# Fourteen warm-up products of 128x128 pieces become twelve steps of four 64x64 pieces over 256 columns

## The chip, the cores and the metric

The kernel runs on one core of a Trainium2 chip. The metric is the device time of one execution in microseconds; lower is better. Before the change the median of three runs is 920.34 us (920.31 to 920.46).

A core has five engines that run side by side and meet only at semaphores: TensorE (PE) for matrix products, VectorE (DVE), ScalarE (ACT), GpSimd (POOL), and SyncE (SP), which here only issues DMA transfers. The profile shows the weight load that goes with each matrix product in a row of its own, PEld.

## What is computed

Two blocks follow each other. The first is an attention in which queries and keys are replaced by products of two small projections; the second sends every row of the result through eight small two-layer networks and mixes their outputs with weights from eight rounds of row and column normalisation.

```python
def phi(x):                       # q, k: (4, 4, 1088, 32); S1, S2: (8, 32)
    a = np.einsum('rd,bhsd->bhsr', S1, x)
    b = np.einsum('rd,bhsd->bhsr', S2, x)
    return np.einsum('bhsi,bhsj->bhsij', a, b).reshape(*x.shape[:-1], r * r)
q_p, k_p = (phi(q), phi(k))
kv = np.einsum('bhsf,bhsd->bhfd', k_p, v)
z = np.sum(k_p, axis=2)
attn = (q_p @ kv) / (q_p . z + 1e-06)          # shortened
...
x = attn as (4352, 128)
P = np.exp(x @ w_gate - max)                   # (4352, 8)
for _ in range(8):
    P /= P.sum(1, keepdims=True) + 1e-09
    P /= P.sum(0, keepdims=True) + 1e-09
    P *= N / E
for e in range(E):                             # w1: (128, 1024), w2: (1024, 128)
    out += P[:, e:e + 1] * (np.maximum(x @ w1[e], 0.0) @ w2[e])
```

All of it is in float32.

## The kernel before

**The large part.** Nearly all the time goes to the eight networks. `first` (the product at L914) multiplies a piece of w1 by up to 512 columns of the transposed activations, in two products that stand beside each other in the array: each has 64 columns of weights, and `tile_position=(0, 0)` or `(0, 64)` says which half of the array's columns it takes. ACT applies the maximum with zero (L918), DVE forms sums and differences (L931, L978), and `into` (L1099) multiplies by w2 or by sums of its pieces. The generator `steps` lays this stream out, and the call `fill(n)` hands out n steps of it between pieces of the attention and of the routing, so that PE has work while those wait.

**The order.** The body of the kernel is recorded inside `tc.manual_schedule`, first for DVE, PE and ACT, then for DVE and PE: on these engines the instructions stand in the order in which they are written. POOL and SP keep the order that the scheduler gives them.

**The start.** Before that body the kernel issues the two small loads of S1 and S2, and POOL fills a 128x128 tile `ones` (L111). PE then runs the loop at L113 and L114: fourteen products of `ones` by `ones` into one PSUM bank, `warm`. Nobody reads `warm`. The tile comes from the pool `aps`, which has four PSUM banks that are handed out in turn (`bank()` takes one, too). POOL clears small tiles, and SP issues the loads of k, q and v.

The first useful work follows in the order of the code at the end of the kernel:

- `projections` (DVE, L34 to L260): turns S1 and S2 into the weights `wd`.
- `transpose_k(0, halves)` (DVE, L302 twice, then L304) and `transpose_q(0, ...)` (DVE, L297): bring k and q into the layout that PE needs.
- `keys_ab(0, halves)` (PE, L314 and L319; ACT, L317 and L320): sixteen products and one more of 64 columns, copied out by ACT into `ab`. `halves` cuts them in two parts of eight, each with a bank of its own; L319 has a third bank.
- `query_products(0)` (PE, L376): four products of 64 rows by 128 columns of weights over 512 columns; two of them stand beside each other in the array's rows, `tile_position=(64 * i, 0)`. Each of the two goes to another PSUM bank.
- `keys_products(0, part)` (DVE, L331): the products of a and b for the keys, into `kp`.
- `keys_sums(0)` (PE, L347): 36 products of `kp` with v; `keys_kept` (ACT, L362) copies them out.
- `fractions(0, ...)` (PE, L392), `queries_ab(1)` (PE, L426), and then the first steps of the large stream.

Queries of later batches go out through DRAM to be repeated: `queries_ab` stores them from SP and POOL (L433, L437), and `repeat_a`, `repeat_b` (SP, L443, L446) load them again as `ph` and `rb`. DVE multiplies these (L453), and PE uses the product at L462.

`logits` (PE, L496) is used further on as a row for comparison: four products of 32 columns of weights each, `tile_position=(0, 32 * b)`, over 512 or 288 columns.

Each float32 product of the code appears in the profile as two weight loads and two matmul instructions; the fourteen products are 28 of each.

Of the kernel before, what the change touches and what calls it, by code (L numbers as in the profile page):

```python
# [10 lines left out]
F32 = mybir.dt.float32  # L11
# [39 lines left out]
def kernel(  # L51
# [12 lines left out]
    nc = tc.nc  # L64
    P = nc.NUM_PARTITIONS
# [19 lines left out]
    aps = ctx.enter_context(tc.tile_pool(name="aps", bufs=4, space=PSUM))  # L85
# [23 lines left out]

    ones = consts.tile([P, P], F32, name="ones")  # L110
    nc.gpsimd.memset(ones, 1.0)  # L111
    warm = aps.tile([P, 512], F32, tag="a", name="a")
    for _ in range(14):  # L113
        nc.tensor.matmul(warm[:, 0:P], ones, ones, start=True, stop=True)  # L114
    own = consts.tile([P, H], F32, name="own")
    nc.gpsimd.memset(own, 0.0)
    for h in range(H):
# [1153 lines left out]
```

## Time and profile before

| | |
|---|---|
| median of three runs | 920.34 us (920.31 to 920.46) |
| the profiled execution, first to last instruction (span) | 918.0 us |
| that execution's own time beyond the span | not given by the profile; the median is 2.3 us above the span |
| PE busy | 911.2 us, 99% of the span |
| DVE busy | 678.9 us, 74% |
| ACT busy | 421.6 us, 46% |
| POOL busy | 204.0 us, 22% |
| the warm-up products at L114 | 28 matmul instructions, starting from 1.0 to 6.9 us |
| start of the first product that uses data (L314) | 7.19 us |

Times within the profile are counted from the first instruction. The busy time of PE says only that some product is in the array: the profile models the ends of matmuls, and two or four products beside each other count once. What a product costs in a dense stream is therefore read from the distance between the starts of equal products. "x8" after a group is the number of instructions in it; of a float32 product these are two. The form "128*64 128x256" means 128 rows by 64 columns of weights, and 256 columns streamed through them.

### The profile page before, as it was taken

Reading aid. Unit: us, or ns where it says so; the run is one execution under the profiler, and the core shown is the slowest. Engines: PE = TensorE matmul, PEld = TensorE weight load, DVE = VectorE, ACT = ScalarE, POOL = GpSimd, SP = SyncE. Lnnn points to the kernel's source line nnn. Section 1 sums busy time; section 2 is a strip of 40 time slices with the busy share of each in tenths; the row PEclk is TensorE's granted clock in tenths of the full one; section 3 lists DMA queues with packets and bytes.
Section 4 is the critical chain, followed back from the end, with each engine's and each line's share of the span. In section 5 each row is a group of like instructions: output and inputs, shape, how many; then the busy total and the mean of one; then the engine's idle time right before and its main releaser. Section 6 shows DMA issues by size and latency. Waiting matters only on the chain.

```text
span 918.0 us, 18893 instructions
## 1 busy us (share of the span) xinstructions
PE 911.2 (99%) x7442; PEld 637.4 (69%) x7442; DVE 678.9 (74%) x1173; ACT 421.6 (46%) x915; POOL 204.0 (22%) x212
## 2 busy tenths in 40 slices
PE   9999999999999999999999999999999999999997
PEld 6777544466666677777777777777777655556886
DVE  7678699888776798666975656956567976758665
ACT  3455555554444454444544444544445444445443
POOL 3121100175545421201210010110100243210220
PEclk9999999999999999999999999999999999999999
DMA  9994100213454535534364343454445456453640
GB/s 254 308 273 163 54 1 1 70 64 127 148 150 139 186 119 174 165 110 150 114 185 134 117 143 112 132 187 127 133 122 165 130 170 195 162 166 92 177 153 13
DMA packets 91305, 128.15 MB, mean 140 GB/s; under 512 B 25392, under 2 KB 69504, under 8 KB 86480
## 3 DMA queue, kind: packets, MB, share of 16 engines
q1 hardware_dynamic: 88384, 121.42, 42.7%
q0 software_dynamic: 1600, 5.36, 2.1%
q8 instruction: 58, 0.95, 0.4%
q10 hardware_dynamic: 1232, 0.16, 0.1%
q14 instruction: 31, 0.25, 0.1%
HBM read 107.88 MB, written 19.05 MB: 138 GB/s over the span
## 4 chain that ended last, share of the span: by engine, by line
PE 97%; DVE 2%; ACT 1%; issue 0%; POOL 0%; DVEq 0%; POOLq 0%
PE a L914 51%; PE s L1099 41%; PE a L347 1%; PE a L462 1%; PE a L114 1%; DVE hb L931 1%; PE a L314 0%; PE s L376 0%; PE a L426 0%; PE s L392 0%; DVE cs L602 0%; PE a L496 0%; PE a L392 0%; ACT hb L918 0%; DVE rs L596 0%
## 5 line engine op out<-in xcount | busy, mean ns | idle before, releaser
L914 PE MATMUL a<-xe,w 128*64 128x256 f32 (+1 forms) x2560 | 569.8, 470 | 0.0
L918 ACT ACTIVATE hb<-a 128x256 f32<-128x256 f32 (+4 forms) x408 | 195.0, 480 | 241.5 <-PE a L914 209.3
L914 PEld LDWEIGHTS a<-xe,w 128*64 128x64 f32 x2560 | 263.0, 137 | 50.8 <-issue 1.8
L918 ACT ACTIVATE hx<-a 128x256 f32<-128x256 f32 (+1 forms) x360 | 167.3, 465 | 213.5 <-PE a L914 191.6
L1099 PE MATMUL s<-hb,ws 128*64 128x256 f32 (+3 forms) x1312 | 256.1, 395 | 0.2 <-DVE hb L931 0.2
L1099 PE MATMUL s<-hx,ws 128*64 128x256 f32 x1280 | 233.9, 379 | 0.0
L978 DVE TENSOR_TENSOR hb<-hb 128x512 f32<-128x512 f32 (+1 forms) x204 | 133.5, 664 | 102.8 <-ACT hb L918 98.8
L978 DVE TENSOR_TENSOR hx<-hx 128x512 f32<-128x512 f32 (+1 forms) x204 | 149.8, 744 | 65.0 <-ACT hx L918 60.2
L1099 PEld LDWEIGHTS s<-hb,ws 128*64 128x64 f32 x1312 | 134.9, 137 | 87.8 <-issue 64.5
L678 POOL TENSOR_TENSOR xe<-xT,xe 128x768 f32<-128x768 f32 (+2 forms) x41 | 80.3, 1958 | 481.2 <-DMA xe<-pT 377.0
L1099 PEld LDWEIGHTS s<-hx,ws 128*64 128x64 f32 x1280 | 132.7, 137 | 71.6 <-issue 50.3
L914 PE MATMUL a<-xT,w 128*64 128x416 f32 (+3 forms) x512 | 119.7, 462 | 0.0
L1099 PE MATMUL s<-hb,w 128*64 128x256 f32 (+3 forms) x536 | 114.2, 408 | 0.0
L1099 PE MATMUL s<-hx,w 128*64 128x256 f32 x384 | 76.0, 379 | 0.0
L931 DVE TENSOR_TENSOR hb<-hb 128x416 f32<-128x416 f32 (+7 forms) x84 | 60.7, 723 | 18.0 <-ACT hb L918 14.0
L1099 PEld LDWEIGHTS s<-hb,w 128*64 128x64 f32 x536 | 54.1, 137 | 19.0 <-issue 6.5
L914 PEld LDWEIGHTS a<-xT,w 128*64 128x64 f32 x512 | 48.9, 137 | 25.5 <-issue 15.7
L242 POOL TENSOR_TENSOR ws<-w 128x256 f32<-128x256 f32 (+1 forms) x70 | 60.5, 899 | 8.1 <-DMA w<-in_moe_w_dram 5.2
L931 DVE TENSOR_TENSOR hx<-hx 128x256 f32<-128x256 f32 (+1 forms) x65 | 39.5, 612 | 24.0 <-ACT hx L918 22.8
L1099 PEld LDWEIGHTS s<-hx,w 128*64 128x64 f32 x384 | 40.8, 137 | 6.6
L978 DVE TENSOR_TENSOR pqg<-hb 128x512 f32<-128x512 f32 x68 | 40.5, 637 | 0.0
L978 DVE TENSOR_TENSOR pqg<-hx 128x512 f32<-128x512 f32 x68 | 35.0, 554 | 0.0
(181 smaller groups left out, 485.0 us busy)
## 6 DMA issues: line engine op xcount, KB each, us to landing
w<-in_moe_w_dram SPq DMA_DIRECT2D x82, 512.0 KB, 5.5
ws<-ws SPq DMA_DIRECT2D x34, 1024.0 KB, 5.0
xe<-pT SPq DMA_DIRECT2D x34, 384.0 KB, 4.1
ws<-ws SPq DMA_DIRECT2D x12, 512.0 KB, 3.6
ph<-qa SPq DMA_DIRECT2D x12, 288.0 KB, 4.7
rb<-qb SPq DMA_DIRECT2D x3, 1152.0 KB, 7.2
pb<-pT SPq DMA_DIRECT2D x6, 384.0 KB, 8.3
kx<-in_k_dram SPq DMA_DIRECT2D x4, 544.0 KB, 4.0
```

What stands on the lines that cost most here:

```text
L114: nc.tensor.matmul(warm[:, 0:P], ones, ones, start=True, stop=True)
L242: tc.keep_in_program_order(nc.gpsimd.tensor_tensor(ws[:, c:c + len(ns)], blocks(x), blocks(y), op=Alu.subtract if off else Alu.add))
L347: nc.tensor.matmul(pv[64 * s:64 * (s + 1), i], kp[0:n, H * t + h].rearrange("p i j -> p (i j)"), vx[0:n, slots[h], t, :], start=(t == 0 an ...
L462: nc.tensor.matmul(pn[64 * s:64 * (s + 1), t, 2 * i:2 * i + 2].rearrange("p h d -> p (h d)"), ph[:, i, s, 64 * t:64 * (t + 1)], kvs[b % 2] ...
L678: tc.keep_in_program_order(nc.gpsimd.tensor_tensor(out, x, pb, op=Alu.mult))
L914: nc.tensor.matmul(ph[sl], loaded_w[j][0][:, P * f + H2 * s:P * f + H2 * (s + 1)], sources[j][:, lo:hi], start=True, stop=True, tile_posit ...
L918: nc.scalar.activation(out=out, in_=ph, func=Act.Relu)
L931: nc.vector.tensor_tensor(out, a, b, op=Alu.subtract)
L978: nc.vector.tensor_tensor(out if not isinstance(out, tuple) else places(*out), places(*a), places(*b) if isinstance(b, tuple) else b, op=A ...
L1099: nc.tensor.matmul(sums[g][i][H2 * s:H2 * (s + 1), n * place:n * (place + 1)], w, x, start=c == 1, stop=c == per, tile_position=(0, H2 * s))
```

## The change

The loop of fourteen products is replaced. Two PSUM banks of `aps` are taken for `warm` instead of one. Twelve steps follow, each of four products: the 64x64 quarters of `ones` are the weights, `tile_position=(64 * r, 64 * c)` puts each quarter in its own quarter of the array, and the columns streamed are 256 copies of the first column of `ones`, read again and again. The two quarters of one row half write to the two halves of the partitions of one bank; the other row half has the other bank. Again nobody reads `warm`.

```diff
     ones = consts.tile([P, P], F32, name="ones")
     nc.gpsimd.memset(ones, 1.0)
-    warm = aps.tile([P, 512], F32, tag="a", name="a")
-    for _ in range(14):
-        nc.tensor.matmul(warm[:, 0:P], ones, ones, start=True, stop=True)
+    warm = [aps.tile([P, 512], F32, tag="a", name="a") for _ in range(2)]
+    for _ in range(12):
+        for r in range(2):
+            for c in range(2):
+                rows, cols = slice(64 * r, 64 * (r + 1)), slice(64 * c, 64 * (c + 1))
+                nc.tensor.matmul(warm[r][cols, 0:256], ones[rows, cols], ones[rows, 0:1].to_broadcast([64, 256]),
+                                 start=True, stop=True, tile_position=(64 * r, 64 * c))
```

In the built program, PE's list has 48 products at this place instead of 14. Every other instruction of every engine stands where it stood. One wait is added: the product at L319, whose bank is now the first of the two of `warm`, waits for PE's own warm-up to have ended.

## The prediction

> **What bounds the kernel.** I read the page first: which engine is full, and what the chain that ended last is made of.
>
> ```profile
> PE 911.2 (99%) x7442; PEld 637.4 (69%) x7442; DVE 678.9 (74%) x1173; ACT 421.6 (46%) x915; POOL 204.0 (22%) x212
> PEclk9999999999999999999999999999999999999999
> PE 97%; DVE 2%; ACT 1%; issue 0%; POOL 0%; DVEq 0%; POOLq 0%
> ```
>
> PE is the bound over the whole span: 97% of the chain lies on it. So a microsecond that PE starts its useful work later is a microsecond at the end, unless PE has a later wait on something that does not move. The chain of waits over the first 11 us shows where that useful work starts:
>
> ```profile
> 0.74 0.20 POOL ones L111
> ...
> 1.00 6.26 PE a L114 x28
> 7.26 1.08 PE a L314 x32
> 8.34 0.11 PE a L319 x2
> 8.45 1.92 PE s L376 x8
> 10.37 2.42 PE a L347 x72
> ```
>
> The 28 warm-up instructions lie on this chain from 1.00 us, and L314 follows them directly. Was L314 waiting for them or for its data? DVE's timeline has the answer:
>
> ```profile
> 5.30 0.35 DVE L260 TENSOR_TENSOR wd<-st,own 128x64 f32<-128x64 f32 x1
> 5.58 1.29 DVE L302 STREAM_TRANSPOSE kT<-kx 128x512 f32<-128x512 f32 x2
> 6.80 0.20 DVE L304 STREAM_TRANSPOSE kT<-kx 128x64 f32<-128x64 f32 x1
> 7.04 0.71 DVE L297 STREAM_TRANSPOSE qT<-qx 128x512 f32<-128x512 f32 x1
> 8.33 1.22 DVE L331 TENSOR_TENSOR kp<-ab 128x1024 f32<-128x1024 f32 x1 [0.58 <-ACT ab L317]
> ```
>
> The weights wd are there at 5.65, the first half of kT at about 6.23, the second at 6.87. PE was the last to be ready. But the gain behind an earlier end is small: L331 cannot start before DVE has finished L297 at 7.75, and it started at 8.33. So an earlier end of the warm-up is worth 0.58 us at most, while a later one costs in full.
>
> **At what pace PE runs.** The clock row prints full speed everywhere, but the products say otherwise at the start:
>
> ```profile
> L114 PE MATMUL a<-ones x28: 341/421/582, 1.0 to 6.9; 128*128 128x128 f32 x28
> 2.65 2.55 PE L114 MATMUL a<-ones 128*128 128x128 f32 x11
> ```
>
> The second line is PE's timeline from 3 to 5 us: eleven instructions fill 2.55 us, of which the last one alone takes 0.42, so ten distances between starts are 2.13 us, 0.213 us for 128 columns. Later 256 columns need hardly more: the chain gives four instructions of L914, two pairs beside each other, 0.43 us, so 0.216 us for 256 columns. The warm-up runs at half the full pace. L314's 16 pairs start from 7.19 to 8.11, 0.06 us a pair for 64 columns, which is nearly the full pace (64/256 of 0.216 is 0.054). The pace doubles about 7 us after the start, and the trace's own clock record bears it out: its first entry, full speed, starts at 7.05 us; the views print 1.00 where there is no entry.
>
> **The change part by part.** Removed: 28 instructions of 0.213 us, all in the open. Added: 48 products, 96 instructions over 256 columns. What four quarters beside each other cost is not in the trace, but two neighbours are. L496 has four products side by side in columns, L376 two side by side in rows:
>
> ```profile
> 106.11 0.64 PE L496 MATMUL a<-xT,wg 128*32 128x512 f32 x4
> ...
> 8.38 0.70 PE L376 MATMUL s<-qT,wq 64*128 64x512 f32 x2
> ```
>
> The first comes from a window of 0.2 us, the second from one of 0.15 us: four, and two, instructions start together; the next four of L496 begin at 106.56, the next pair of L376 at 8.92, then 9.35, 9.77, so 0.42 to 0.45 us for 512 columns, the pace of a single stream. Columns and rows both overlap, so I take four-fold overlap: 96 instructions are 24 groups of 256 columns, each 0.427 us at the half pace (twice 0.213) and 0.216 at the full. From the other side: if only two of the four overlap, there are 48 groups. Neither row is like that, so I take 24 and keep 48 as a rival.
>
> The moment of the doubled pace is the second unknown. Between bounds: at the start of the products (24 x 0.216 = 5.2 us, end at 6.2 us, before the data, so 0.58 us gained) and never during them (24 x 0.427 = 10.2 us). The nearest row is L114 itself, an array as full as the new one, from the same start: doubling at 7.05 us. The sum: first start 1.00; the first instruction took 0.16 us longer than its successors (1.00 to 1.37), so 1.16. Until 7.05: 5.89 / 0.427 = 13.8 groups. Left: 10.2 groups at 0.216 = 2.2 us, to 9.25. The turn from row halves to column halves costs about 0.10 us (L376's last pair at 9.77 plus 0.43, L347 at 10.30), so L314 starts at 9.35 instead of 7.19: 2.16 us later.
>
> What does the delay meet? Behind the warm-up on PE stand L314, L319, L376; ACT waits for L314 to fill ab, DVE for ab (L331), PE's L347 for kp, ACT for L347, PE's L392 for ACT (a wait of 0.6 us): each of these is released by the one before, so they all move by the same amount. Stores and reloads of ab through DRAM (L433 to L446) move as a whole, too, as do the loads queued behind them on SP; the ones ahead of them do not move and finish relatively earlier, so DMA can only be less in the way. On PE's own list of waits there are 0.6 us for ACT, 0.2 for DVE and the 1.0 at the start; none is for a transfer with a fixed date, so nothing takes the 2.16 us back. I cost the remaining edits at nothing: the second bank is taken from four when none of the others is in use, which turns the later hand-outs by one place; the wait added to L319 is for products that ended sixteen products earlier on the same engine. If that cover failed, the price would be one drain, 0.1 us.
>
> Sum, on the profiled execution: 918.0 + 2.2 = 920.2 us; the median of the runs lies 2.3 us higher, so 922.5.
>
> Two rules of the Trainium skill speak against the change. The page "TensorE: Matmul & The Clock Gate", Part 1, says the clock is lifted after a busy window of 3.413 us that runs freely, so it is a matter of time and not of the number of products. The clock record agrees in one point: it lasts 911.36 us, 267.0 such windows. By that page alone the doubling could come, by the phase of the window, between about 4.4 and 7.8 us (one to two windows after the first start), and my sum would lie between +0.9 and +2.5 us; as an estimate it makes the spread wider, not its sign. The same page, Part 3, says a weight load overlaps a running product only in another row group; by that, one load in each group would stand in the open, 24 x 0.14 = 3.3 us more. The row of L914, loads of 137 ns and still 0.43 us for four, shows no such cost.
>
> **The rivals.** (1) The clock rises earlier, since four weight sets and two streams for each row half look busier than one. For it: nothing in this trace excludes that the measure counts tiles. Against it: the array is as full in L114. Price with the doubling half way, at 4.0 us: 6.7 groups by then, 17.3 x 0.216 = 3.74, end at 7.74, L314 at 7.84: +0.65 us, 921.0, not slower by 0.2%. It decides from a doubling before about 6.4 us, where the sum falls under 1.84 us. (2) The pieces do not lift the clock while they run: end at 1.16 + 10.2 = 11.4 us, L314 at 11.5, +4.3 us, 924.6; and if the work behind needed another 6 us at half pace, 3 us on top, 927.6. Against it is the full array again. (3) The quarters overlap only in twos: 48 groups, 34.2 left at 7.05 us, 7.4 us, end at 14.4, L314 at 14.5, +7.3, 927.6. Against it: both rows above. (4) The change does nothing, because a later wait takes the delay: for it speak only short waits of ACT and DVE after 130 us; 920.3 to 921.
>
> **How the numbers follow.** A measurement of this kernel tells 0.2% from no change, 1.84 us. My forecast, doubling near 7 us with four-fold overlap, gets 0.60, with its own range 921.6 to 922.9 (a doubling between 5.2 and 7.9 us: 0.49 us later for each microsecond); 0.50 of it lies above 922.18, since the row that fixes 7.05 is a direct one. Rival 1 gets 0.25, rival 2 0.07, rival 3 0.05, rival 4 0.03. Slower by more: 0.50 + 0.07 + 0.05 = 0.62. Within: 0.10 + 0.25 + 0.01 = 0.36. Faster by more would need 1.84 us where the data allow 0.58; I leave 0.02 (out of rival 4) for what I do not see. The range 920.8 to 924.7 leaves out rival 3, the long half of rival 2 and the earliest part of rival 1, some 0.15.
>
> **What would show it.** In the profile after: 96 instructions at the warm-up's line, starting in fours; 0.43 us between fours until about 7 us and 0.22 after; last start near 9.0; L314 at 9.3 to 9.4, L331 at about 10.5. The span is 920.2, and the products after 166 us take as long as before. A first start of L314 near 7.8 with fours 0.22 us apart from 4 us on is rival 1; fours that never come closer than 0.43 us are rival 2; pairs are rival 3. If L314 is 2 us late and the span is not, the statement that nothing takes it back was wrong.

## The result: 1.1 us slower, half of what was forecast

Over 18 runs of each, the changed kernel takes 921.30 us in the median (920.16 to 925.5) and the kernel before 920.23 us (919.18 to 921.34). The ratio is 1.0015 with a 95% interval of 1.0009 to 1.0021: slower beyond doubt, by 1.1 us, which is less than the 0.2% that was called measurable and half of the 2.16 us of the forecast. The time lies in the range that was given.

The page of the changed kernel, its parts 1 and 2, against the rows shown of before:

```profile
PE 913.1 (99%) x7510; PEld 596.8 (65%) x7510; DVE 685.0 (74%) x1173; ACT 421.2 (46%) x915; POOL 211.0 (23%) x212
PEclk9999999999999999999999999999999999999999
```

PE is as full as before; the span has grown from 918.0 to 919.9 us. The chain of waits of the changed kernel (start, length, what; lines have moved down by four: L117 is the warm-up, L318 was L314, L380 was L376, L351 was L347):

```profile
1.00 8.17 PE a L117 x96
9.16 1.08 PE a L318 x32
...
10.36 1.92 PE s L380 x8
12.28 2.42 PE a L351 x72
```

The warm-up holds 8.17 us of the chain instead of 6.26. The products behind it have their old lengths and stand 1.9 us later: L318 starts at 9.10 instead of 7.19. The same 1.9 us are between the two traces at the first product of the large stream (19.31 against 17.41), at its last (914.55 against 912.65) and at the end (919.9 against 918.0); on the way the distance varies by a few tenths (2.0 at L462, which starts at 36.02 against 34.04). Nothing took it back in this execution.

PE's timeline of the changed kernel, from two windows (4.4 to 6.2 us, 6.59 to 8.6 us); a group also holds the instructions that still run when the window opens:

```profile
4.04 2.73 PE L117 MATMUL a<-ones 64*64 64x256 f32 x24
...
6.17 2.78 PE L117 MATMUL a<-ones 64*64 64x256 f32 x44
```

The 24 instructions of the first line are six fours with starts from 4.04 to 6.17, 0.427 us apart; within a four the starts lie at most 0.02 us apart, so all four quarters run at once. The 44 of the second line are eleven fours; from 6.60 on they are 0.22 us apart. The trace's clock record starts at 6.59 us.

DVE's timeline of the changed kernel holds something that the profile of before did not show:

```profile
6.71 1.30 DVE L306 STREAM_TRANSPOSE kT<-kx 128x512 f32<-128x512 f32 x2 [1.06 <-DMA kx<-in_k_dram]
7.93 0.20 DVE L308 STREAM_TRANSPOSE kT<-kx 128x64 f32<-128x64 f32 x1
8.06 0.67 DVE L301 STREAM_TRANSPOSE qT<-qx 128x512 f32<-128x512 f32 x1
```

The load of k came 1.06 us later than DVE was ready for it; before, DVE started at 5.58 with no wait. No instruction of that load was changed. In the changed kernel this cost nothing, since L318 still had to wait for the warm-up.

### The profile page after: what moved, and what is told of

Same layout as the page of the kernel before. It is cut to its first block, busy times and chain, and to the rows that moved or that the text cites. A ratio compares the mean times of both kernels' runs of the same rounds, so it can differ in the third digit from the quotient of the medians.

```text
span 919.9 us, 19030 instructions
## 1 busy us (share of the span) xinstructions
PE 913.1 (99%) x7510; PEld 596.8 (65%) x7510; DVE 685.0 (74%) x1173; ACT 421.2 (46%) x915; POOL 211.0 (23%) x212
## 4 chain that ended last, share of the span: by engine, by line
PE 98%; DVE 1%; issue 0%; ACT 0%; POOL 0%; DVEq 0%; POOLq 0%
PE a L918 56%; PE s L1103 37%; PE a L351 1%; PE a L117 1%; PE a L466 1%; PE a L318 0%; PE s L380 0%; DVE hb L935 0%; PE a L430 0%; PE s L396 0%; PE a L500 0%; PE a L396 0%; DVE cs L606 0%; DVE rs L600 0%; DVE y L794 0%
## 5 line engine op out<-in xcount | busy, mean ns | idle before, releaser
L918 PE MATMUL a<-xe,w 128*64 128x256 f32 (+1 forms) x2560 | 692.1, 470 | 0.0
L918 PEld LDWEIGHTS a<-xe,w 128*64 128x64 f32 x2560 | 320.4, 137 | 112.8 <-issue 1.6
L1103 PE MATMUL s<-hb,ws 128*64 128x256 f32 (+3 forms) x1312 | 331.6, 395 | 0.2 <-DVE hb L935 0.2
L1103 PE MATMUL s<-hx,ws 128*64 128x256 f32 x1280 | 306.3, 379 | 0.0
L1103 PEld LDWEIGHTS s<-hb,ws 128*64 128x64 f32 x1312 | 158.4, 137 | 70.2 <-issue 14.2
L1103 PEld LDWEIGHTS s<-hx,ws 128*64 128x64 f32 x1280 | 154.5, 137 | 57.3
L1103 PE MATMUL s<-hb,w 128*64 128x256 f32 (+3 forms) x536 | 134.4, 408 | 0.0
L1103 PE MATMUL s<-hx,w 128*64 128x256 f32 x384 | 95.7, 380 | 0.0
L1103 PEld LDWEIGHTS s<-hb,w 128*64 128x64 f32 x536 | 60.5, 137 | 23.4 <-issue 6.5
L982 DVE TENSOR_TENSOR pqg<-hb 128x512 f32<-128x512 f32 x68 | 46.5, 723 | 0.0
```

The lines of the kernel that those rows point to most:

```text
L918: nc.tensor.matmul(ph[sl], loaded_w[j][0][:, P * f + H2 * s:P * f + H2 * (s + 1)], sources[j][:, lo:hi], start=True, stop=True, tile_posit ...
L982: nc.vector.tensor_tensor(out if not isinstance(out, tuple) else places(*out), places(*a), places(*b) if isinstance(b, tuple) else b, op=A ...
L1103: nc.tensor.matmul(sums[g][i][H2 * s:H2 * (s + 1), n * place:n * (place + 1)], w, x, start=c == 1, stop=c == per, tile_position=(0, H2 * s))
```

## The experiments

Twelve runs were made on four chips, and each group had its own runs of the kernel before beside it. "Moment" is the time at which the trace's clock record begins, the doubled pace; "first" is the start of the first useful product (L314 of before). The median includes what lies outside the span of an execution, the time from its first to its last instruction.

| run | against the kernel before | median, us | moment | first |
|---|---|---|---|---|
| e1, changed kernel again | 1.0012 (1.0003 to 1.0021) | 921.48 | 6.48 | 9.04 |
| e2, seven steps of quarters | 1.0009 (0.9998 to 1.0020) | 921.00 | 4.81 | 6.41 |
| e3, twelve whole products of 256 columns | 1.0008 (1.0000 to 1.0017) | 921.15 | 5.58 | 8.64 |
| e4, no warm-up | 1.0017 (1.0007 to 1.0027) | 921.60 | 12.54 | 7.11 |
| e5, kernel before again | 0.9999 (0.9991 to 1.0008) | 920.20 | 5.14 | 7.02 |
| e6, before, k later | 1.0013 (1.0004 to 1.0022) | 921.02 | 4.20 | 8.17 |
| e7, changed, k later | 1.0014 (1.0005 to 1.0023) | 921.48 | 7.06 | 9.32 |
| e8, twenty-four steps | 1.0070 (1.0058 to 1.0083) | 926.76 | 4.87 | 13.48 |
| e9, before, k in two halves | 1.0010 (1.0002 to 1.0019) | 920.86 | 5.07 | 7.49 |
| e10, the same, eleven products | 1.0014 (1.0005 to 1.0023) | 921.71 | 5.11, and again 11.94 | 8.82 |
| e11, seven steps of quarters again | 1.0010 (1.0001 to 1.0019) | 921.07 | 5.67 | 6.96 |
| e12, seven whole products of 256 columns | 1.0001 (0.9992 to 1.0010) | 920.28 | 5.09 | 6.48 |

**e1, the changed kernel again.** No edit.

> The changed kernel once more, as the yardstick for the other runs of this chip. Theory of length (the warm-up costs the time that PE spends in it beyond the moment when k and q are ready; what kind of product fills it does not matter): 0.9 to 1.5 us over the kernel before; the start of the first useful product is 0.49 times the moment of the doubled pace plus 5.87 us, so between 8.0 and 9.8 us, with the moment between 4.4 and 7.9 us. Theory of kind (the quarters themselves lift the clock later, or turn the array at a price): the same time, but the moment would often lie beyond 7.9 us.

1.06 us over the kernel before, as in the first measurement. The formula of the expectation is the sum of the forecast with the moment left open. The moment is 6.48 us, and 0.49 x 6.48 + 5.87 gives 9.05 us for the first product; it started at 9.04.

**e2 and e11, seven steps of quarters**, as long at the half pace as the fourteen products:

```diff
-    for _ in range(12):
+    for _ in range(7):
```

> Only the number of steps differs from the changed kernel: seven steps of four quarters, 14 groups of 0.427 us at the half pace, 5.97 us, the same as the fourteen whole products of the kernel before. Theory of length: the time of the kernel before, within 0.3 us. Theory of kind: most of the loss stays, 0.7 to 1.1 us over the kernel before.

> The seven steps of quarters once more, since their interval held both theories. Theory of length: the time of the kernel before, ratio 1.000 within 0.0006. Theory of kind: ratio 1.0009 to 1.0015, as the twelve steps.

The medians are 0.6 and 0.9 us over the kernel before. The first interval holds both theories, the second just leaves out no change. By the medians the theory of length was missed twice, and the theory of kind was met in e11 and just missed in e2.

The spans on record say otherwise. Their medians are 918.9 and 918.7 us, in both runs 0.3 over the kernel before on the same chip (918.6 and 918.4), which the theory of length allows. The rest lies outside the span: 2.0 to 3.0 us in eight of these 22 executions, where the other fourteen and every execution of the kernel before have 1.7 to 1.9.

The two traces, too, show nothing of the quarters in the start: the first products began at 6.41 and 6.96 us, after the warm-up had ended and as soon as kT was there, earlier than the 7.19 of the kernel before. What e11's profiled execution lost, it lost elsewhere, most of it at the last stores: its last product of the large stream starts at 913.02 us and the end comes 6.3 us later, where the other traces have 5.3 to 5.4. The four last stores of ACT's queue, in before and in e11, take 1.91 and 2.96 us to issue:

```profile
913.56 1.91 ACTq L872 DMA_DIRECT2D out_dram<-yt  x4
```

```profile
913.93 2.96 ACTq L876 DMA_DIRECT2D out_dram<-yt  x4
```

**e3, whole products as long as the twelve steps:**

```diff
-    for _ in range(14):
-        nc.tensor.matmul(warm[:, 0:P], ones, ones, start=True, stop=True)
+    for _ in range(12):
+        nc.tensor.matmul(warm[:, 0:256], ones, ones[:, 0:1].to_broadcast([P, 256]), start=True, stop=True)
```

> Only the length differs from the kernel before: twelve whole products of 128x128 over 256 columns, 24 instructions of 0.427 us at the half pace, as long as the twelve steps of quarters. Theory of length: the time of the changed kernel, within 0.3 us (0.8 to 1.4 us over the kernel before). Theory of kind: the time of the kernel before, within 0.3 us.

The chain of e3, in the kernel's old line numbers:

```profile
0.99 7.71 PE a L114 x24
8.71 1.08 PE a L314 x32
```

The moment was 5.58 us, the sum 0.49 x 5.58 + 5.87 gives 8.6 us, and L314 started at 8.64: a quarter of the instructions, the same length. The median is 0.7 us over the kernel before, just under what was expected, and its interval begins at no change.

**e4, no warm-up**, the loop and `warm` left out:

> The warm-up is left out; what it computed was read by nobody. Theory of length: the first useful product starts when k is ready, at 6.3 to 7.4 us, and runs at half the pace until the clock rises, which PE's activity from there on brings about 3.4 to 7 us later; about half of that is lost: 1 to 3.5 us over the kernel before, and the doubled pace is seen only after 10 us. If the kernel before had its clock from somewhere else than the warm-up: 0 to 0.6 us faster than the kernel before.

```profile
1.51 4.81 DMA kx<-in_k_dram
...
6.34 0.72 DVE kT L299
...
7.11 1.97 PE a L311 x32
9.08 0.21 PE a L316 x2
9.29 3.55 PE s L373 x8
```

Here the chain is the load of k. The 32 instructions of the first product's line take 1.97 us instead of 1.08 and the eight of the next take 3.55 instead of 1.92: half the pace, until the moment at 12.54 us. The cost is 1.2 us. So fourteen products are worth 1.2 us, and twelve steps of quarters give back nearly all of it: with 921.48 us on the same chip their median is only 0.1 us better than without a warm-up.

**e5, the kernel before against itself.** No edit.

> The kernel before against itself, for the noise and for a second look at its start. Ratio 1.000 within 0.001. Theory of two spreads (the moment of the doubled pace lies anywhere between about 4.4 and 7.9 us, and the load of k lands up to 1.1 us later in some executions): the profile's own moment of the doubled pace will not be 7.05 us again, and the first useful product starts between 6.3 and 8.0 us, set by whichever ends last of the warm-up and the load. If both are fixed to the start of the kernel: 7.05 us and 7.19 us again, within 0.05.

Its chain:

```profile
1.50 4.72 DMA kx<-in_k_dram
...
6.25 0.72 DVE kT L302
...
7.02 1.28 PE a L314 x32
```

The same program, and another start: the moment at 5.14 us instead of 7.05, the warm-up over 0.7 us before L314, and L314 set by the load of k, which landed at 6.23. In the first profile of this kernel, k was there before 5.58 and the warm-up was the last to end. Both are spreads of single executions, not properties of the kernel.

The earlier start did not make e5 shorter: its span is 918.4 us against 918.0. The turning of q on DVE (L297) comes behind that of k, and the next products (L376, L347) stand where they stood before, within 0.04 us. Then the repeated queries come back through DRAM 0.5 us later than in the first profile, and L462 stands 0.35 us later. Before, and then e5:

```profile
32.79 1.83 DVE L453 TENSOR_TENSOR ph<-ph,rb 128x768 f32<-128x768 f32 x2 [4.56 <-DMA rb<-qb]
34.04 0.87 PE L462 MATMUL a<-kvs,ph 128*64 128x66 f32 x24
```

```profile
33.33 1.83 DVE L453 TENSOR_TENSOR ph<-ph,rb 128x768 f32<-128x768 f32 x2 [5.06 <-DMA rb<-qb]
34.39 0.92 PE L462 MATMUL a<-kvs,ph 128*64 128x66 f32 x24
```

**e6 and e7, k issued after the first piece of q**, in the kernel before and in the changed one:

```diff
-    load_k(0)
     load_q(0, 0, 16)
+    load_k(0)
```

> The kernel before with the first piece of q issued ahead of k, so that k lands 0.5 to 1.3 us later. Theory (in the kernel before, a late k is in the open): 0.3 to 1.2 us over the kernel before, and the first useful product waits for k. If k has slack there: no change, within 0.2 us.

> The changed kernel with the same exchange of loads. Theory (the long warm-up hides a late k, so part of what it costs was already lost in the kernel before): the time of the changed kernel, 0.9 to 1.4 us over the kernel before and within 0.3 us of it; the first useful product starts right after the warm-up, at 0.49 times the moment of the doubled pace plus 5.87 us. If the late k added to it: 1.5 to 2.5 us over the kernel before.

The chain of e6, and then, from another view, the chain of e7:

```profile
2.35 5.03 DMA kx<-in_k_dram
...
7.40 0.72 DVE kT L302
...
8.17 1.28 PE a L314 x32
```

```profile
1.00 8.40 PE a L117 x96
9.39 1.08 PE a L318 x32
```

In both, DVE had k at 7.4 us. The kernel before pays for it, 1.0 us in the median, with L314 at 8.17. The changed kernel does not show it at its start, with the warm-up alone on the chain: its long warm-up covers a late k. Its median is 1.4 us over the kernel before of this chip, at the upper edge of what was expected, where e1 has 1.1 on its chip; the two intervals overlap. This execution also answers the forecast directly: its moment is 7.06 us, the value that the forecast assumed, and L318 starts at 9.32 where 9.35 was forecast; the span is 920.2 us, as forecast.

**e8, twice the steps**, `range(24)`:

> Twice the steps. Theory of length: the twelve steps more all run at the full pace, 24 groups of 0.216 us, 5.2 us over the changed kernel and 6.1 to 6.7 us over the kernel before; the first useful product at 0.49 times the moment of the doubled pace plus 11.05 us. If later waits take back part of a late start of PE: clearly less, 3 to 5 us.

```profile
1.00 12.55 PE a L117 x192
13.55 1.08 PE a L318 x32
```

Moment 4.87 us, 0.49 x 4.87 + 11.05 = 13.4, and L318 started at 13.48. Against e1's profile the first product starts 4.4 us later and the span ends 4.5 us later (924.6 against 920.0). The median of five executions is 6.7 us over the kernel before, 5.3 over the 921.48 of e1 and of e7 where the sum gives 5.2; two of the five have 0.5 and 1.0 us of it outside the span. A long delay of PE's start goes to the end in full.

**e9 and e10, the first k in two halves from two queues**, an attempt at a faster kernel:

```diff
-    load_k(0)
+    kx0 = ld.tile([P, SA, D], F32, tag="k", name="kx", bufs=1)
+    for i, queue in enumerate((nc.sync, nc.scalar)):
+        queue.dma_start(out=kx0[64 * i:64 * (i + 1)],
+                        in_=k[0, 2 * i:2 * (i + 1)].rearrange("h (s a) d -> (h s) a d", a=SA))
+    loaded["k", 0] = kx0
```

> The kernel before with its load of the first k in two halves, one from SP and one from ACT's queue, so that k is issued 0.4 us sooner. Theory (the first useful product of the kernel before waits in many executions for k): k lands 0.2 to 0.8 us earlier and the time falls by 0.2 to 0.6 us. If the transfer is bound by the DMA engines and not by its issue: no change, within 0.2 us.

> The same with eleven whole products instead of fourteen, 4.7 us at the half pace, an end at 5.85 us at the latest. Theory of length: with an early k, the first useful product starts at 6.3 to 6.4 us, 0.3 to 0.9 us under the kernel before. Against it: where the doubled pace comes after 5.85 us the work behind runs up to 1 us at the half pace, which gives back up to 0.5 us.

DVE's timelines of e9 and of e10:

```profile
6.72 1.31 DVE L306 STREAM_TRANSPOSE kT<-kx 128x512 f32<-128x512 f32 x2 [1.07 <-DMA kx<-in_k_dram]
```

```profile
8.05 1.30 DVE L306 STREAM_TRANSPOSE kT<-kx 128x512 f32<-128x512 f32 x2 [2.18 <-DMA kx<-in_k_dram]
```

Both expectations failed. In the timelines SP's half takes 0.81 us to issue, as long as the whole k did in e5 (0.80), so this half was issued no sooner; ACT's half was, by 0.3 us (1.43 + 0.61 against 1.50 + 0.80). k landed no earlier, at about 6.7 and 8.0 us. In e10 that puts the first product at 8.82 us.

e10's profiled execution, the slowest of its eleven (922.87 us), shows what a warm-up that ends long before the data risks. PE was done with it at 5.67 us and stood idle for 3.15 us. The clock record falls back to half speed at 8.53 us and returns to full at 11.94, so the first useful products run at half the pace, 1.98 us instead of 1.08 (a row for 9 to 11 us, in which the third number from the end is the clock, and a row of the chain):

```profile
9.00:11.00 2.00, 2.00 (x36) 1.88 (x35) 1.68 (x4) 0.53 (x2) 0.00 (x0) 0.50 1.18 227
```

```profile
8.82 1.98 PE a L318 x32
```

So e10 does not price eleven products with an early k. No kernel tried here beats the kernel before.

**e12, seven whole products of 256 columns**, e3 with `range(7)`:

> Seven whole products of 128x128 over 256 columns: the kind of the kernel before in the length of the seven steps of quarters, which is also the length of the fourteen products (5.97 us at the half pace). If the 0.6 to 0.9 us of the seven steps come from the quarters: the time of the kernel before, ratio 1.000 within 0.0006. If they come from the form over 256 columns, or from whatever differs between any two programs here and is not on PE: ratio 1.0006 to 1.0012, as the seven steps of quarters. Theory of length alone: 1.000.

The time of the kernel before within 0.1%: by the medians the expectation that blames the quarters for the 0.6 to 0.9 us was met, and so was that of length alone. The spans do not blame the quarters, since the median span, 918.5 us, is 0.3 over that of the kernel before (918.2), as with the seven steps of quarters. Its trace, in PE's waits and DVE's timeline, shows the wait before L462 larger than e5 had it:

```profile
PE a L462 <- issue: 1.3, 1, 1.3
```

```profile
33.96 1.83 DVE L453 TENSOR_TENSOR ph<-ph,rb 128x768 f32<-128x768 f32 x2 [6.23 <-DMA rb<-qb]
```

The first product began 0.7 us earlier than in the first profile of the kernel before, but the queries that come back through DRAM (rb) came 1.2 us later than there (33.96 against 32.79), and PE stood 1.3 us before L462. The early start was lost there.

## Why the forecast was right in kind and twice too large

**What bounds the kernel: right, for that execution.** PE is the bound, a later start goes to the end in full (1.9 us at the start and at the end of the profile after; 4.4 and 4.5 us between e1 and e8). The sentence "PE was the last to be ready" was read from one execution: in e5 the load of k was last, and PE waited 0.7 us for it.

**Pace and overlap: right.** Fours start together, 0.427 us apart at the half pace and 0.22 at the full. Rival 3, overlap in twos, is excluded.

**The moment of the doubled pace: mis-sized.** The forecast took "doubling at 7.05 us" from "the nearest row", L114 of one execution. In the thirteen traces that have a warm-up the moment lies between 4.20 and 7.06 us, 5.6 in the mean; 7.05 is the second latest of them. The working behind it holds: first start = 0.49 x moment + 5.87 was met within 0.05 us in the four traces of twelve long steps or products (9.10, 9.04, 8.64, 9.32). At 5.6 us it gives 8.6, 1.4 us later than 7.19 and not 2.16: 0.7 us too much in the sum. That the forecast's 9.35 was met almost exactly in e7 is luck: its moment fell at 7.06.

**The base: mis-sized, too.** The forecast added 2.3 us for what lies around the span, the median less the profiled span. But those belong to different executions. Where one execution has both numbers, the difference is 1.7 to 1.9 us (921.71 and 919.9; in e5 920.20 and 918.4), but for ten executions with seven or 24 steps of quarters. By this the profiled execution of before was one of some 919.8 us, 0.4 under the median of 18: unlike e5 and e12, it lost nothing before L462. Put together, 918.0 + 1.8 + 1.4 = 921.2 us, where 921.3 was measured; that the two agree so closely is partly luck, since the base is a fortunate execution.

**That "a later one costs in full": true of the profiled pair, less for the medians.** In the profiles of kernels whose first product starts between 6.4 and 7.5 us (before, e2, e5, e9, e11, e12), the stretch from there to the end of the span takes 910.8, 911.2, 911.4, 911.8, 912.3 and 912.4 us. In those that start at 8.2 us or later and at the full clock (after, e1, e3, e6, e7, e8) it takes 910.7 to 911.1. An early start is thus partly lost again, in e5 and e12 at L462, so the changed kernel gives up less than its later start. With one trace each this is a reading of single executions, not a measured share of the 1.1 us.

**Rival 1, an earlier clock by the quarters.** An earlier moment came, but not by the quarters: those with quarters have 4.81, 4.87, 5.67, 6.48, 6.59, 7.06 us, those with whole products 4.20, 5.07, 5.09, 5.11, 5.14, 5.58, 7.05. Rival 2, a clock that does not rise during the pieces, was seen in none. Rival 4 is excluded by the profile after as the whole account, although e5 and e12 show that such a wait exists in some executions.

**The rules of the Trainium skill.** The forecast set the rule of "TensorE: Matmul & The Clock Gate", Part 1, of a window that runs freely, beside the sum as a matter of spread. The runs side with the rule: the moment is not tied to the kernel's start, 7.05 and 5.14 us in two executions of the same program. Twelve of the thirteen moments lie in the 4.4 to 7.8 us that the forecast estimated from it; e6's 4.20 lies just below. At the middle of that range, 6.1, the sum is 1.7 us. The rule of Part 3, weight loads that overlap only across row groups, is not seen here: e1's fours stand 0.22 us apart at the full pace, with no load in the open.

**What stays open.** By the spans, which are recorded to 0.1 us, seven steps of quarters and seven whole products cost the same, 0.3 us over the kernel before. By the medians the quarters have 0.6 and 0.9 us and the whole products 0.3, because of the executions with 2 to 3 us outside the span. Only kernels with seven or 24 steps of quarters have these; none of the 41 executions of the changed kernel, with or without a late k, does. Where that time comes from was not tried. That the length costs is shown by the starts of e1, e3, e7 and e8, and by the time of e8; how the 1.1 us divide is not. e3, as long as the twelve steps but of whole products, has 0.7 us where they have 1.1 on the same chip, with overlapping intervals.

## What to carry to other kernels

A warm-up of the array is worth its length only up to the moment when the data are there: here fourteen products gain 1.2 us over none, and a warm-up about 2 us longer gives that back. Too short is a risk as well: where the data came 3 us after its end, the clock had fallen again (e10). Before a forecast of a microsecond, ask which numbers of a single profile would be others in the next execution, such as the phase of the clock and the landing of the first loads, and take the middle of their spread and not the one row. And find the time beyond the span from an execution that has both numbers, since the median and the profile may belong to different ones.

## What the runs showed of the hardware

The clock record at full speed lasts 907.945, 911.359, 914.772 or 918.185 us in these traces: steps of 3.413 us whatever the length of the kernel. In e10 two records of 3.413 us, one full and one half, come first. With moments of 7.05 and 5.14 us in one and the same program, this says that the clock changes only at ticks that the kernel does not start. Counted back from the moment in such steps, e6's clock rose at 4.20 us, after a tick in which PE was busy from 1.00 us on, 94% of it; in the kernel before, the tick from 0.22 to 3.63 us was busy for 77% and was not enough. It fell in e10 after a tick that was busy for 16% (5.11 to 8.53 us), and stayed in e6 through one that was busy for half (4.20 to 7.61). The clock's column in the profile prints full speed at the start, where there is no record yet, although the products run at half the pace.

On SP, half of the load of k takes as long to issue as the whole, 0.81 us against 0.80. And k in two halves from two queues landed at 6.7 and 8.0 us. As one piece and in the old order it was there at 6.7 us at the latest in ten traces, in three of them by 5.7. Why was not tried.
